# Attention block with SwiGLU: per-group storage of queries and keys, earlier first maxima, a three-tile operation order and a GpSimd split of the maxima

## The chip, the cores and the metric

The kernel runs on one NeuronCore of a Trainium2 chip. The metric is the device time of one execution in microseconds; before the change the median of three runs is 2182.06 us (2181.04 to 2183.07).

The engines named below are TensorE (PE in the profile; its weight loads are PEld), VectorE (DVE), ScalarE (ACT), GpSimd (POOL) and SyncE (SP, which here only issues DMAs).

## The reference

One pre-norm transformer block on 2048 tokens of width 640, with 32 heads of 20 dimensions and a SwiGLU feed-forward of width 1728, all in float32:

```python
h  = x + attention(layernorm(x)) @ wo        # qkv = layernorm(x) @ wqkv; scores * 20 ** -0.5; softmax
h2 = h + (silu(n @ w_gate) * (n @ w_up)) @ w_down      # n = layernorm(h)
```

The softmax subtracts the row maximum. The output is `h2`, 1 x 2048 x 640.

## The kernel before, in words

**Precision.** Most matrix products are made from float32r operands that are split into a high part and a remainder (`split`: ScalarE rounds, VectorE or GpSimd subtracts). A projection is then the sum of three products.

**Projection stage.** Tokens go in four chunks of 512 (`c` = 0 to 3). Each chunk has 18 slots: ten blocks of 128 query or key dimensions (`query_key`, 15 matmuls of 512 columns each) and eight value parts (`value`, 15 matmuls of 320 columns). The last chunk does its five key blocks, then the values, then its five query blocks. `keep` copies a finished block to the tile `e` (two buffers), splits it there on ScalarE and GpSimd, and stores it to DRAM (`qk_d`) from ScalarE's DMA queue, one block behind. The layernorm of the next chunk runs on VectorE between the slots, and `flip` turns it into `z_hi` and `z_lo`.

**Heads and units.** Heads go in eight groups of four. A unit `u` is one group and one chunk of 512 queries, so there are 32. Two heads of a group lie in the lower 64 partitions and two in the upper (`b` = 0, 1), so a score matmul occupies one half of TensorE's rows. Keys and queries of a group are stacked from `qk_d` by `stack`, four DMAs each on SyncE's queue: `load_keys`, `load_queries`, and `load_staged`, which puts a copy into `raw` tiles for early use.

**Row maxima.** Before a unit's scores can be made, the maximum of each query over all 2048 keys is needed. Each maximum is a score matmul followed by a reduction on VectorE. In the projection stage a wide maximum covers both halves at once (`max_pair`: two matmuls into `ps_wide`, one reduction of 128 x 1024). In the attention stage a single maximum covers one half (`max_one`: one matmul into `ps_max`, three banks, one reduction of 128 x 512). `visit(n)` starts up to `n` wide maxima that are ready at the end of a slot; the lists `urgent` and `early` hold them with the slot from which they are allowed. `rest` lists what is left for the attention stage. There are 168 wide maxima and 1712 single ones.

When a unit's maxima are complete, `max_all` reduces them over the key chunks with the sign turned, and `max_finish` transposes them on TensorE, splits the result into two float32r parts on VectorE and writes these by four DMAs into spare rows of the unit's query tile. The score matmul then subtracts the maximum by itself.

**Attention stage.** Each unit walks over 16 key tiles of 128. A tile makes four scores with exponentials (`scores`: one matmul into `ps_one`, four banks, one activation) and weighs the values of the tile two before (`weigh`). The operations of a tile are an order written out by hand: `s` and `S` are scores of the lower and upper half, `m` and `M` single maxima of the lower and upper half, `W` is the weighting. The order alternates between two tiles, and upper and lower case are exchanged in every second pair.

```python
ORDER = ("ssmSWS", "mMsMsWSmMmS")
```

At the end of a unit, the weighted sums are copied, divided by the row sums and stored (`row_sums`, `reciprocals`, `spread`, `store_o`). The output projections of the first chunks run inside the last two units. The feed-forward stage follows.

Of the kernel before, what the change touches and what calls it, by code (L numbers as in the profile page):

```python
# [14 lines left out]
ALU = mybir.AluOpType  # L15
# [21 lines left out]
EPS = 1e-5  # L37

ORDER = ("ssmSWS", "mMsMsWSmMmS")
# [3 lines left out]
def tile_block(ctx: ExitStack, tc: tile.TileContext, x, wqkv, wo, wg, wu, wd, out):  # L43
# [6 lines left out]
    qk_d = dram.tile([2, 2, D, S], F32R, name="qk_d")  # L50
# [59 lines left out]
    def stack(dst, which, g, cs):  # L110

        src = qk_d[which].bitcast(F32).rearrange("i (d h) c -> (i d) h c", h=H)
        for b in range(2):
            heads = src[:, g * G + b : (g + 1) * G : 2, cs]
# [50 lines left out]
    def max_all(u):  # L165
        ends[u] = stk.tile([P, G * TPC], F32, name="neg", tag="neg", bufs=2)
        nc.vector.tensor_reduce(
            ends[u], mxs[u].rearrange("p b h t k -> p (b h t) k"), axis=AX.X, op=ALU.max,
            negate=True,
        )  # L170

    def max_finish(u):

        m = ps_one()[: G * TPC, :P]
        nc.tensor.transpose(m, ends.pop(u), ident)
        m2 = stk.tile([G * TPC, 2, P], F32R, name="m2", tag="m2", bufs=1)
        nc.vector.tensor_copy(m2[:, 0], m)
        nc.vector.tensor_tensor(out=m2[:, 1], in0=m, in1=m2[:, 0].bitcast(F32), op=ALU.subtract)
        for b in range(2):
            for i in range(2):  # L180
                row = b * ROW + NPART + i
                nc.sync.dma_start(
                    queries[u][row : row + 1].bitcast(F32).rearrange(
                        "r j (t p) -> r (j t) p", t=TPC
                    ),
                    m2[b * 2 * TPC : (b + 1) * 2 * TPC, i, :].bitcast(F32),
                )

# [6 lines left out]
        for kc in range(2 if u == 2 else 1 if u % NC < 2 else 0, NC)  # L195
        for t in range(TPC)
        for pair in range(2)
    ]
# [5 lines left out]
    with tc.tile_pool(name="pa", bufs=2) as pa:  # L204
# [31 lines left out]
        def load_staged(i):  # L236
            g, c = sets[i]
            k, q = stage_tile(), stage_tile()
            stack(k, 1, g, slice(0, CH))
            stack(q, 0, g, slice(c * CH, (c + 1) * CH))  # L240
            staged[i] = q, k

        def load_next(i):
            if i < len(sets):
                if slot[0] + 1 >= ready_at(sets[i][1]):
                    load_staged(i)
                else:
                    waiting_load.append(i)

        def first_keys(i, t, pair):  # L250
            if t == 0 and pair == 0:
                load_next(i + 1)
            max_pair(mxs[sets[i][0] * NC + sets[i][1]], *staged[i], pair, t, 0, 0)
# [6 lines left out]
        def in_unit(u, kc, at):  # L260
            return [
                (at, lambda t=t, pair=pair: unit_keys(u, kc, t, pair))
                for t in range(TPC) for pair in range(2)
            ]

        def in_set(i):
            return [
                (ready_at(sets[i][1]), lambda t=t, pair=pair: first_keys(i, t, pair))
                for t in range(TPC) for pair in range(2)
            ]  # L270

        urgent = [a for kc in range(NC) for a in in_unit(0, kc, 18 * kc + (14 if kc == 0 else 8))]
        early = [a for i in range(NG - 1) for a in in_set(i)]
        early += in_unit(1, 0, ready_at(1))
        early += [a for i in range(NG - 1, len(sets)) for a in in_set(i)]
        early += in_unit(2, 0, ready_at(2)) + in_unit(2, 1, ready_at(2))

        def visit(n):
            if waiting_load and slot[0] + 1 >= ready_at(sets[waiting_load[0]][1]):
                load_staged(waiting_load.pop())  # L280
# [8 lines left out]
        def load_w(i):  # L289

            m, n = blocks[i]
# [53 lines left out]
        def store(*last, queue=nc.scalar):  # L345

            if stores:
                queue.dma_start(*stores.pop())
            if last:
                stores.append(last)  # L350

        def query_key(c, *ms):

            z_hi, z_lo = zs[c]
            pss = [ps_one() for _ in ms]
            n = 0
            for a, w in ((z_hi, w_hi), (z_lo, w_hi), (z_hi, w_lo)):
                for ps, m in zip(pss, ms):
                    for k in range(ND):
                        nc.tensor.matmul(  # L360
                            ps, w[:, k, m * P : (m + 1) * P], a[:, k, :],
                            start=(n == 0 and k == 0), stop=(n == 2 and k == ND - 1),
                        )
                n += 1
            for ps, m in zip(pss, ms):
                keep(c, m, ps)

        def keep(c, m, ps):
            e = evp.tile([P, 2, CH], F32R, name="e")
            split_sbuf(ps, e[:, 0], e[:, 1], e[:, 1].bitcast(F32))  # L370
            dst = qk_d[m // ND].bitcast(F32).rearrange("i r c -> r i c")
            store(dst[(m % ND) * P : (m % ND + 1) * P, :, c * CH : (c + 1) * CH], e.bitcast(F32))

        def value(c, t, half):
# [16 lines left out]
            if half == 1:  # L391
                rows = slice((c * TPC + t) * P, (c * TPC + t + 1) * P)
                store(v_d[rows], ev)
            else:
                store()
# [3 lines left out]
        order = [5, 6, 7, 8, 9, 0, 1, 2, 3, 4, 10, 11, 12, 13, 14]  # L399
        blocks = [(5, 2), (7, 2), (9, 1), (0, 2), (2, 2), (4, 1), (10, 2), (12, 2), (14, 1)]  # L400
# [7 lines left out]
        first_raw = raws.pop(order[0]), raws.pop(order[1])  # L408
        for i, raw in enumerate(first_raw):
            cs = slice(order[i] * P, (order[i] + 1) * P)  # L410
            nc.scalar.activation(w_hi[:, :, cs], raw, AF.Copy)
        for t in range(TPC):
            flip_tokens(t)
        for i, raw in enumerate(first_raw):
            cs = slice(order[i] * P, (order[i] + 1) * P)
# [8 lines left out]
        keys_first = [("block", m) for m in order[:ND]]  # L424
        first = [("block", *order[:2]), ("none",), *keys_first[2:]]
        queries_next = [("block", m) for m in order[ND : 2 * ND]]
        flip_at = (12, 11, 11)
        finish_at = 18 * NC
        for c in range(NC):
            lns = []  # L430
            work = (keys_first if c else first) + queries_next + parts
            if c == NC - 1:
                work = keys_first + parts + queries_next
            for j, (kind, *which) in enumerate(work):
                slot[0] = 18 * c + j
                if c == 0 and j < 9:
                    for i in range(split_at[j], split_at[j + 1]):
                        m = order[i + 2]
                        split_w(m)
                        if loaded < len(blocks) and m == sum(blocks[loaded - 4]) - 1:  # L440
                            load_w(loaded)
                            loaded += 1
# [6 lines left out]
                visit(3)  # L449
                if c == 0 and j == 11:  # L450
                    load_staged(0)
# [3 lines left out]
                if j == (7 if c == 0 else 5):  # L455
                    load_keys(0, slice(c * CH, (c + 1) * CH))
                if j == 10 and c < 3:
                    load_queries(c)
# [193 lines left out]
    todo, tail, accs, closing = [], [], {}, []  # L652
# [21 lines left out]
    for u in range(NU):  # L674
# [4 lines left out]
        for kt in range(NT):  # L679
            ready, closing[:] = closing[:], []  # L680
# [262 lines left out]
```

## Time and profile before

| quantity | value |
|---|---|
| median of three runs | 2182.06 us (2181.04 to 2183.07) |
| the profiled execution | 2184.13 us |
| its span, first to last instruction | 2182.3 us |
| projection stage, to the first exponential | 312.4 us |
| attention stage, first to last exponential | 312.4 to 1565.5 us |
| steady attention unit (16 tiles) | 37.54 to 37.67 us |
| units 0, 1, 30 | 39.7, 38.7, 62.7 us |
| granted TensorE clock | 0.998 |

All durations come from one profiled execution. The time of that execution is 1.8 us above its span and 2.1 us above the median. The busy time of an engine counts an instruction from its start to its modelled end; neighbouring instructions overlap, so the mean duration in a row is longer than the distance at which two of them follow each other. Lines such as L161 are line numbers of the kernel before.

### The profile page before, as it was taken

Reading aid. Unit: us, or ns where it says so; the run is one execution under the profiler, and the core shown is the slowest. Engines: PE = TensorE matmul, PEld = TensorE weight load, DVE = VectorE, ACT = ScalarE, POOL = GpSimd, SP = SyncE. Lnnn points to the kernel's source line nnn. Section 1 sums busy time; section 2 is a strip of 40 time slices with the busy share of each in tenths; the row PEclk is TensorE's granted clock in tenths of the full one; section 3 lists DMA queues with packets and bytes.
Section 4 is the critical chain, followed back from the end, with each engine's and each line's share of the span. In section 5 each row is a group of like instructions: output and inputs, shape, how many; then the busy total and the mean of one; then the engine's idle time right before and its main releaser. Section 6 shows DMA issues by size and latency. Waiting matters only on the chain.

```text
span 2182.3 us, 33646 instructions
## 1 busy us (share of the span) xinstructions
PE 2148.1 (98%) x12882; PEld 1250.8 (57%) x12882; DVE 1640.5 (75%) x2835; ACT 1312.8 (60%) x2454; POOL 302.6 (14%) x218
## 2 busy tenths in 40 slices
PE   7999999999999999999999999999999999999999
PEld 5776763333333333333333333345688888888888
DVE  6699879999999999999999999974353343453444
ACT  4322238999999999999999999976622111121110
POOL 5222220000000000000000001011213222122220
PEclk9999999999999999999999999999999999999999
DMA  6555421211102102112111012011221000010102
GB/s 205 193 174 196 162 99 30 58 36 55 47 22 62 43 19 78 27 41 64 34 57 45 24 58 77 19 58 57 73 63 40 25 25 25 19 31 19 31 19 97
DMA packets 120864, 136.60 MB, mean 63 GB/s; under 512 B 37440, under 2 KB 71104, under 8 KB 120704
## 3 DMA queue, kind: packets, MB, share of 16 engines
q1 hardware_dynamic: 107600, 107.71, 17.0%
q10 hardware_dynamic: 13104, 26.75, 3.4%
q8 instruction: 101, 1.65, 0.3%
q14 instruction: 59, 0.48, 0.1%
HBM read 95.62 MB, written 38.01 MB: 61 GB/s over the span
## 4 chain that ended last, share of the span: by engine, by line
PE 88%; DVE 6%; DMA 4%; ACT 1%; issue 0%; SPq 0%; POOL 0%; ACTq 0%; DVEq 0%; POOLq 0%
PE acc L610 22%; PE ps_one L600 18%; PE ps_a L794 17%; PE ps_max L155 11%; PE ps_b L880 9%; PE ps_one L360 4%; DVE mx L161 2%; DVE mx L149 2%; DMA qk_d<-e 2%; PE ps_one L382 2%; PE ps_max L540 2%; PE ps_wide L145 2%; PE ps_b L540 1%; ACT e L217 0%; DMA wo_raw<-in_A_wo 0%
## 5 line engine op out<-in xcount | busy, mean ns | idle before, releaser
L606 ACT ACTIVATE probs<-ps_one 128x512 f32<-128x512 f32 x2048 | 1080.7, 601 | 142.5 <-PE ps_max L155 86.8
L161 DVE TENSOR_REDUCE mx<-ps_max 128x1 f32<-128x512 f32 x1712 | 1067.4, 683 | 64.7 <-PE ps_max L155 58.5
L600 PE MATMUL ps_one<-q_stk,k_stk 62*128 62x512 f32 x2048 | 682.6, 445 | 2.6 <-ACT probs L606 1.0
L155 PE MATMUL ps_max<-k_stk,q_stk 60*128 60x512 f32 x1712 | 609.4, 439 | 4.7 <-DVE mx L161 1.5
L600 PEld LDWEIGHTS ps_one<-q_stk,k_stk 62*128 62x128 f32 x2048 | 338.1, 184 | 413.5 <-ACT probs L606 362.8
L610 PE MATMUL acc<-probs,v_stk 128*32 128x512 f32 x4096 | 547.0, 606 | 0.0
L885 DVE TENSOR_TENSOR h<-ps_b,h 128x320 f32<-128x320 f32 x448 | 194.6, 486 | 311.9 <-PE ps_b L880 311.8
L155 PEld LDWEIGHTS ps_max<-k_stk,q_stk 60*128 60x128 f32 x1712 | 277.8, 185 | 142.2 <-DVE mx L161 119.9
L794 PE MATMUL ps_a<-z,gu_hi 128*128 128x512 f32 x1080 | 276.0, 393 | 0.6 <-ACT z L71 0.6
L794 PEld LDWEIGHTS ps_a<-z,gu_hi 128*128 128x128 f32 x1080 | 200.4, 188 | 42.2 <-ACT z L71 0.8
L149 DVE TENSOR_REDUCE mx<-ps_wide 128x2 f32<-128x1024 f32 x168 | 194.6, 1219 | 33.2 <-PE ps_wide L145 32.8
L71 ACT ACTIVATE y_hi<-s 128x512 fp32r<-128x512 f32 (+1 forms) x56 | 35.4, 631 | 253.9 <-DVE s L807 247.5
L645 POOL TENSOR_TENSOR o<-o,rb 128x512 f32<-128x512 f32 x31 | 39.8, 1284 | 1032.0 <-DMA q_stk<-qk_d 642.7
L610 PEld LDWEIGHTS acc<-probs,v_stk 128*32 128x32 f32 x4096 | 80.7, 108 | 157.7 <-issue 149.5
L802 ACT ACTIVATE s<-ps_a 128x512 f32<-128x512 f32 (+1 forms) x56 | 33.5, 598 | 199.4 <-PE ps_a L794 199.4
L794 PE MATMUL ps_a<-z,gu_lo 128*128 128x512 f32 x540 | 142.2, 393 | 0.0
L880 PE MATMUL ps_b<-d_hi,y_hi 128*128 128x320 f32 x448 | 139.0, 311 | 0.0
L880 PE MATMUL ps_b<-d_lo,y_hi 128*128 128x320 f32 x448 | 138.1, 309 | 0.0
L880 PE MATMUL ps_b<-d_hi,y_lo 128*128 128x320 f32 x416 | 128.3, 308 | 0.0
L217 ACT ACTIVATE e<-ps_one 128x512 f32<-128x512 f32 x55 | 32.9, 598 | 150.4 <-DMA qk_d<-e 74.6
L794 PEld LDWEIGHTS ps_a<-z,gu_lo 128*128 128x128 f32 x540 | 101.4, 188 | 23.1
L72 POOL TENSOR_TENSOR y_lo<-s,y_hi 128x512 fp32r<-128x512 f32 x52 | 67.8, 1303 | 269.6 <-ACT y_hi L71 269.6
(109 smaller groups left out, 1535.4 us busy)
## 6 DMA issues: line engine op xcount, KB each, us to landing
qk_d<-e ACTq DMA_DIRECT2D x39, 512.0 KB
k_stk<-qk_d SPq DMA_DIRECT2D x64, 160.0 KB
q_stk<-qk_d SPq DMA_DIRECT2D x64, 160.0 KB
raw<-qk_d SPq DMA_DIRECT2D x56, 160.0 KB
rb<-r_d SPq DMA_DIRECT2D x32, 256.0 KB
v_d<-ev ACTq DMA_DIRECT2D x16, 384.0 KB
v_stk<-v_d SPq DMA_DIRECT2D x28, 192.0 KB
xt<-in_A_x SPq DMA_DIRECT2D x16, 320.0 KB
```

What stands on the lines that cost most here:

```text
L72: lo_engine.tensor_tensor(out=lo, in0=src, in1=hi.bitcast(F32), op=ALU.subtract)
L149: nc.vector.tensor_reduce(mx[:, :, pair, t, kc], ps, axis=AX.X, op=ALU.max)
L155: nc.tensor.matmul(ps, queries[u][rows, pair, t * P : (t + 1) * P], keys[u // NC][rows, pair, kc * CH : (kc + 1) * CH], start=True, stop=True,
L161: nc.vector.tensor_reduce(mxs[u][:, b, pair, t, kc : kc + 1], ps, axis=AX.X, op=ALU.max)
L360: nc.tensor.matmul(ps, w[:, k, m * P : (m + 1) * P], a[:, k, :], start=(n == 0 and k == 0), stop=(n == 2 and k == ND - 1),)
L540: nc.tensor.matmul(ps[:, :HALF], a[:, k, :], w[:, k, hs], start=(n == 0), stop=(n == 3 * ND - 1),)
L600: nc.tensor.matmul(ps, keys[u // NC][rows, p, kt * P : (kt + 1) * P], queries[u][rows, p, :], start=True, stop=True,)
L606: nc.scalar.activation(probs[p][:, b, :], ps, AF.Exp, scale=scale)
L610: nc.tensor.matmul(acc[32 * j : 32 * j + 32, :], values[u // NC][:, kt, j * VW : j * VW + 32], probs[j // 2][:, j % 2, :], start=(kt == 0) ...
L794: nc.tensor.matmul(ps, a[:, i, k, :], b[:, k, :], start=(n == 0), stop=(n == 3 * ND - 1))
L880: nc.tensor.matmul(ps[:, :HALF], a[:, t * P : (t + 1) * P], b[:, hs], start=(n == 0), stop=(n == len(products) - 1),)
L885: nc.vector.tensor_tensor(out=h, in0=ps[:, :HALF], in1=h, op=ALU.add)
```

## The change

1. `qk_d` is laid out by head group, so that a group's 80 query or key dimensions are contiguous. The columns of `wqkv` are permuted on the host to match, and query and key blocks alternate. A block of 128 dimensions then lies in two or three groups and is stored in two or three pieces.
2. The first wide maxima are allowed from slot 6 instead of 14, per group (`ready_at`). `visit` is called with two in the middle of a block and two after it, instead of three after it; value slots keep three. Unit `c = 1` of each group also does part of its second key chunk early (`in_projections`). Staged sets are 21 instead of 14. In the built program there are 208 wide maxima and 1632 single ones.
3. In chunk 0 every third block uses `third`, a view of the value tile, as an additional `e` buffer.
4. The attention order has three tiles, without the exchange of case; when no maxima are left it is `sSsSW`. Finished maxima are transposed two tiles after they close instead of one.
5. The split of a finished maximum happens before the transpose on GpSimd (`max_all`: a copy and a subtraction of 128 x 16); after the transpose one ScalarE copy takes the place of the two VectorE operations.

```diff
-ORDER = ("ssmSWS", "mMsMsWSmMmS")
+GD = G * DH
+ORDER = ("SmsSMMsWMm", "SsSmWmMs", "SssMWmS")
...
-    qk_d = dram.tile([2, 2, D, S], F32R, name="qk_d")
+    qk_d = dram.tile([2, NG, 2, GD, S], F32R, name="qk_d")
...
     def max_all(u):
-        ends[u] = stk.tile([P, G * TPC], F32, name="neg", tag="neg", bufs=2)
+        neg = stk.tile([P, G * TPC], F32, name="neg", tag="neg", bufs=2)
         nc.vector.tensor_reduce(
...
+        ends[u] = stk.tile([P, 2, G * TPC], F32R, name="both", tag="both", bufs=2)
+        nc.gpsimd.tensor_copy(ends[u][:, 0], neg)
+        nc.gpsimd.tensor_tensor(
+            out=ends[u][:, 1], in0=neg, in1=ends[u][:, 0].bitcast(F32), op=ALU.subtract
+        )
     def max_finish(u):
-        nc.tensor.transpose(m, ends.pop(u), ident)
-        m2 = stk.tile([G * TPC, 2, P], F32R, name="m2", tag="m2", bufs=1)
-        nc.vector.tensor_copy(m2[:, 0], m)
-        nc.vector.tensor_tensor(out=m2[:, 1], in0=m, in1=m2[:, 0].bitcast(F32), op=ALU.subtract)
+        nc.tensor.transpose(m, ends.pop(u).bitcast(F32).rearrange("p i n -> p (i n)"), ident)
+        m2 = stk.tile([2 * G * TPC, P], F32R, name="m2", tag="m2", bufs=1)
+        nc.scalar.activation(m2, m, AF.Copy)
...
+    def in_projections(u, kc, t):
+        g, c = divmod(u, NC)
+        if u == 0 or (u == 2 and kc < 2) or (c < 2 and kc == 0):
+            return True
+        return c == 1 and kc == 1 and t < (2 if g < NG // 2 else 3)
...
-        sets = [(g, c) for c in range(2) for g in range(1, NG)]
-        def ready_at(c):
-            return 18 * c + 14
+        sets = [(g, 0, 0) for g in range(1, NG)]
+        sets += [(g, 1, kc) for g in range(1, NG) for kc in range(2)]
+        def ready_at(g, c):
+            block = ((g + 1) * GD - 1) // P
+            return 2 * block + 6 if c == 0 else 18 * c + 9 + block
...
         def query_key(c, *ms):
...
+                        if n == 1 and k == 3:
+                            visit(2)
...
         def keep(c, m, ps):
-            e = evp.tile([P, 2, CH], F32R, name="e")
+            if c == 0 and m % 3 == 2:
+                e = third.bitcast(F32R)
+            else:
+                e = evp.tile([P, 2, CH], F32R, name="e")
...
-                visit(3)
+                visit(2 if kind == "block" else 3)
...
-                closing.append(a[0])
+                closing[a[0]] = now[0] + 2
...
-            for op in ORDER[kt % 2]:
-                if kt % 4 >= 2 and op != "W":
-                    op = op.swapcase()
+            order = ORDER[now[0] % 3] if singles[0] or singles[1] else "sSsSW"
+            for op in order:
```

More of the change, by code (lines that the diff above doesn't have):

```diff
@@ L194, in tile_block @@
         for u in range(1, NU)
-        for kc in range(2 if u == 2 else 1 if u % NC < 2 else 0, NC)
+        for kc in range(NC)
         for t in range(TPC)
         for pair in range(2)
+        if not in_projections(u, kc, t)
     ]
@@ L244, in load_next, with load_waiting @@
             if i < len(sets):
[L245 to L248, printed above, removed]
+                waiting_load.append(i)
+                load_waiting()
+        def load_waiting():
+            if waiting_load and slot[0] + 1 >= ready_at(*sets[waiting_load[0]][:2]):
+                load_staged(waiting_load.pop())
         def first_keys(i, t, pair):
@@ L252, in first_keys @@
                 load_next(i + 1)
-            max_pair(mxs[sets[i][0] * NC + sets[i][1]], *staged[i], pair, t, 0, 0)
+            g, c, kc = sets[i]
+            max_pair(mxs[g * NC + c], *staged[i], pair, t, kc, 0)
         def unit_keys(u, kc, t, pair):
@@ L345, in store @@
         def store(*last, queue=nc.scalar):
[L347 to L350, printed above, removed]
+            while stores:
+                queue.dma_start(*stores.pop(0))
+            stores.extend(last)
         def query_key(c, *ms):
@@ L392, in value @@
                 rows = slice((c * TPC + t) * P, (c * TPC + t + 1) * P)
-                store(v_d[rows], ev)
+                store((v_d[rows], ev))
             else:
@@ L407, in tile_block @@
             f()
[L408 to L411, printed above, removed]
+        first_raw = raws.pop(0), raws.pop(1)
+        for m, raw in enumerate(first_raw):
+            nc.scalar.activation(w_hi[:, :, m * P : (m + 1) * P], raw, AF.Copy)
         for t in range(TPC):
             flip_tokens(t)
-        for i, raw in enumerate(first_raw):
-            cs = slice(order[i] * P, (order[i] + 1) * P)
+        for m, raw in enumerate(first_raw):
+            cs = slice(m * P, (m + 1) * P)
             nc.vector.tensor_tensor(
@@ L423, in tile_block @@
         parts = [("value", *divmod(i, 2)) for i in range(2 * TPC)]
-        keys_first = [("block", m) for m in order[:ND]]
-        first = [("block", *order[:2]), ("none",), *keys_first[2:]]
-        queries_next = [("block", m) for m in order[ND : 2 * ND]]
+        first = [("block", 0, 1), ("none",)] + [("block", m) for m in range(2, 2 * ND)]
+        some_keys = [("block", 2 * i) for i in range(ND)]
+        some_queries = [("block", 2 * i + 1) for i in range(ND)]
         flip_at = (12, 11, 11)
@@ L437, in tile_block @@
                     for i in range(split_at[j], split_at[j + 1]):
-                        m = order[i + 2]
-                        split_w(m)
-                        if loaded < len(blocks) and m == sum(blocks[loaded - 4]) - 1:
+                        split_w(i + 2)
+                        if i % 2 == 1 and loaded < 8:
                             load_w(loaded)
@@ L650, in store_o @@
             )
-    todo, tail, accs, closing = [], [], {}, []
+    todo, tail, accs, closing, now = [], [], {}, {}, [0]
     singles = [[(*a, b) for a in rest] for b in range(2)]
```

73 lines of the change are left out of this document (44 added, 29 removed).

## The prediction

> **What bounds the kernel now.** I read the totals first, then the busy time stage by stage, then single starts inside the two stages that the diff touches. The feed-forward stage (from 1565.5 us on) keeps its instructions and is taken as unchanged.
>
> ```profile
> span 2182.3 us, 33646 instructions
> ...
> PE 2148.1 (98%) x12882; PEld 1250.8 (57%) x12882; DVE 1640.5 (75%) x2835; ACT 1312.8 (60%) x2454; POOL 302.6 (14%) x218
> ```
>
> Busy time by stretch (columns: span, PE, PEld, DVE, ACT, POOL, clock, DMA share, GB/s): two token chunks of the projections, 30 attention units, units 30 and 31.
>
> ```profile
> 84.50:162.60 78.10, 76.10 (x399) 56.23 (x399) 72.72 (x85) 21.86 (x38) 19.35 (x15) 1.00 0.56 181
> 162.60:239.40 76.80, 75.39 (x400) 55.98 (x399) 72.40 (x85) 21.97 (x38) 19.34 (x15) 1.00 0.56 183
> 312.40:1446.00 1133.60, 1129.47 (x7457) 430.36 (x7453) 1070.15 (x1798) 1030.49 (x1957) 54.79 (x38) 1.00 0.17 47
> 1446.00:1508.70 62.70, 60.02 (x366) 32.88 (x364) 37.22 (x84) 39.05 (x79) 7.60 (x5) 1.00 0.16 50
> 1508.70:1565.50 56.80, 56.70 (x340) 31.13 (x341) 16.93 (x47) 38.66 (x78) 7.58 (x5) 1.00 0.11 32
> ```
>
> In both stages TensorE (PE) and VectorE (DVE) are both nearly full. Moving maxima forward therefore relieves one full stage and loads another. The timeline (start, length, count) within one old two-tile cycle shows what holds attention:
>
> ```profile
> 703.11 1.06 PE L610 MATMUL acc<-probs,v_stk 128*32 128x512 f32 x8
> 704.11 0.49 PE L600 MATMUL ps_one<-q_stk,k_stk 62*128 62x512 f32 x1
> 704.11 1.11 PE L155 MATMUL ps_max<-k_stk,q_stk 60*128 60x512 f32 x3
> 704.72 1.20 PE L600 MATMUL ps_one<-q_stk,k_stk 62*128 62x512 f32 x4
> ```
>
> VectorE beside it:
>
> ```profile
> 702.78 4.38 DVE L161 TENSOR_REDUCE mx<-ps_max 128x1 f32<-128x512 f32 x7
> 707.42 2.58 DVE L161 TENSOR_REDUCE mx<-ps_max 128x1 f32<-128x512 f32 x4 [0.26 <-PE ps_max L155]
> ```
>
> VectorE runs seven reductions back to back, then starves. TensorE waits too: the third maximum behind the weighting at 703.11 starts at 704.72, when the reduction begun at 703.98 gives back one of three `ps_max` banks. Both idle in turn because the old order puts one maximum into one tile and six into the next.
>
> **Attention, steady tiles.** Starts of single rows give the rules. Weighting (W) to the next matmul takes 1.00 us, the first step to the second 0.34, later steps 0.235, the last step to W 0.32. A step holds one matmul on each row half (s, m lower; S, M upper), since neighbours on different halves start together. Reductions follow at 0.60 and begin 0.56 after an interval's first matmul; a bank is free 0.75 after its reduction begins. Exponentials follow at 0.48.
>
> Old order, without waits: three steps (1.00 + 0.34 + 0.235 + 0.32 = 1.90) and five steps (2.37), so 4.27 for two tiles. Measured, W to W, are 1.90 and 2.74 (703.11 to 705.85), sum 4.64: 0.38 is the bank wait with the weight load that it exposes (0.11).
>
> New order, W to W: `m S, S m, s S, M, M s` is five steps, 2.37; `M m, S s, S m` three, 1.90; `m M, s S, s, s M` four, 2.13. Sum 6.40 for three tiles, 2.13 a tile: TensorE's own work per tile is as before. Maxima per interval are 4, 3 and 3 instead of bunched. The fourth in the long interval is the one that waits: the first has its matmul at 1.00, its reduction at 1.56, its bank back at 2.31, where the fourth could start at 2.05. That is 0.26, plus up to 0.11 of exposed weight load. Three in the other intervals find free banks (the third of the last comes at 1.81, its bank 0.3 earlier). VectorE needs 10 x 0.60 = 6.0, ScalarE 12 x 0.48 = 5.8: neither is the bound. I take 6.70, between 6.66 and 6.77.
>
> A unit is 16 tiles: 16/3 x 6.70 = 35.7. Old units take 37.65, which is 8 x 4.64 + 0.52; I keep the 0.52 though two VectorE operations (L177 and L178, 0.28 each) leave it. New unit 36.2, a gain of 1.45 x 30 units = **43 us**. Bounds: no waits at all (34.6) 92 us; old rate kept 2 us.
>
> The ScalarE copy that replaces those operations has no row: 0.20 (the one-column activation L471) to 0.60 (L217), I take 0.3, 9 us over 31 units in a stage where ScalarE idles 103; the exponentials queue behind it and have four banks of cover. The two small GpSimd operations are bounded by nothing and 1.3 us (its 512-column rows): GpSimd is busy 55 of 1134 us, and the transpose now comes two tiles (4.5 us) after the last maximum, so I take zero. If GpSimd were late, the transpose on TensorE and everything behind it would stand. Each unit's rows still arrive in time: unit 1 has 40 single maxima left, closes in tile 11, is transposed in tile 13, needed in tile 16; four DMA issues of 0.65 and a landing fit into that.
>
> **Attention, last two units.** After the maxima end (tile 489, both orders) the new order is `sSsSW`. With an output projection (2.40) a tile takes 1.00 + 2.40 + 0.34 + 0.32 = 4.06; the old pair took 9.06 (W at 1508.92, 1517.98). Eight tiles gain 3.8. Some 14 light tiles go from 2.13 towards the exponentials' 1.92: 2.5. Unit 30's eight projection tiles with maxima go from 5.14 (1456.51 to 1466.78 for two) to about (6.40 + 7.2 + 0.9)/3 = 4.83: 2.4. Together **9 us**, bounds 3 to 13.
>
> **Projections: 40 wide maxima more (168 to 208), 80 single ones fewer.**
>
> ```profile
> L149 DVE TENSOR_REDUCE mx<-ps_wide 128x2 f32<-128x1024 f32 x168 | 194.6, 1219 | 33.2 <-PE ps_wide L145 32.8
> ```
>
> One slot of the timeline (start, length):
>
> ```profile
> 87.51 0.62 PE L360 MATMUL ps_one<-z_hi,w_lo 128*128 128x512 f32 x2
> 88.06 0.96 PE L145 MATMUL ps_wide<-raw 60*128 60x512 f32 x6
> ...
> 92.60 0.97 PE L145 MATMUL ps_wide<-raw 60*128 60x512 f32 x6
> ```
>
> VectorE takes a wide maximum every 1.14. A block slot here (88.06 to 92.60) is 4.55: 15 matmuls at 0.229, three wides at 0.229, and 0.40 for entering and leaving half-array matmuls. Four wides in two visits make 3.44 + 0.92 + 0.80 = 5.16. The built order has 88 such excursions against 56. TensorE's price is 40 x 0.229 + 32 x 0.40 = 22 us.
>
> The Trainium skill ("TensorEngine Tiling (Array Packing)", Key Properties) says that changing the tiling mode drains TensorE, which speaks against splitting the visits. The rows show it cheaper than a full drain: the wide at 88.06 starts before the end of the matmul ahead (87.51 + 0.62 = 88.13). Waiting for both ends would make 0.53 an excursion and 4 us more; no run here shows such a wait, and the sum below uses the rows.
>
> By chunk, wides are 12, 54, 54, 48 before and 40, 60, 64, 44 after. In chunks 1 and 2 VectorE is the fuller engine once wides are added (72.7 + 6.8, 72.4 + 11.4 busy), so these grow by **7 and 11**. Chunk 0 gets 28 more: four block slots at about 5.9 (four wides 4.56, plus weight splits and layernorm steps that took 0.6 to 2.2 each there) and eight value slots at 3.6, less the 4.8 that TensorE waited for stores, which a third `e` buffer ends: end near 91 instead of 84.5, **+6.5**. Chunk 3 has four fewer wides but more excursions, and five final blocks at the pace of their stores:
>
> ```profile
> ACT e L217 <- DMA qk_d<-e: 74.6, 23, 4.7
> ```
>
> (us, times, longest, from 16 to 312 us.) In the chain, the landing of a staged load and of a store:
>
> ```profile
> 147.89 3.13 DMA raw<-qk_d
> ...
> 304.85 2.75 DMA qk_d<-e
> ```
>
> A store becomes two or three pieces, 96 issues against 40, 0.37 each on ScalarE's queue, with the next copy behind them: harmless at a 5.2 slot, up to 0.5 a block in the tail. Chunk 3: **+4.5**.
>
> Staged sets are 21 instead of 14, 56 more issues of 0.34 on SyncE. A set's eight issues and a landing of 3.1 make 5.8. Eight wides last 10 us and hide it; three sets of four wides last 5.2 and miss by 0.6; four sets of six hide it. **+2**; with the longest landing in the chain (6.2) 15 instead. Sum **+31**. Low end 17: TensorE's 22 less 4.8. High end 46.
>
> **Sum.** 31 - 43 - 9 = -21. The profiled execution (2184.1, span 2182.3) would become 2163; it lies 2 above the median of 2182.1, so the median becomes **2161**.
>
> **Rivals.**
> *Bank waits vanish.* For: 4/3/3 spacing, VectorE at 6.0 of 6.4. Against: three banks, four maxima in one interval. 31 - 92 - 9 = -70: 2112. Chance 0.12.
> *Wides cost only TensorE's share* (visits spaced so that VectorE never holds it): 17 - 52 = -35: 2147. Against: VectorE at 94% in chunk 2 already. Chance 0.12.
> *Staged loads late.* DMA already moves 181 GB/s in these chunks and SyncE's queue is in order, so a load that waits for a store holds those behind it. With landings of 6.2: -8; a little more brings it level: 2174 to 2182. Chance 0.12.
> *Slower: scores wait for their banks.* The long interval issues five scores in 1.3 us into four `ps_one` banks; the fourth needs the bank of the last score before W, free at 1.78, where it could start at 1.58. That is hidden behind the maximum's wait only while ScalarE keeps pace. From 0.2 more in each cycle (6.93) attention returns no more than the projections take; at the old rate, 2.32 a tile, it is 31 - 2 - 9 = +20: 2202. For: exponentials run 10 to 15% short of bound, so any copy queued ahead shows. Chance 0.13.
> The counts (208 and 1632) stand in the built order, so a change that does not do what it says is given nothing.
>
> **How the numbers follow.** The forecast case keeps 0.51, itself 2150 to 2175. 0.2% is 4.4 us, about what a measurement of this kernel can tell from no change. Faster by more: the forecast's 0.51, 0.12 + 0.12, and 0.04 of the late loads: 0.79. Same: the other 0.08. Slower: 0.13. The range leaves out part of each outer case: 2122 to 2190.
>
> **What would show it.** Right: attention starts near 343 instead of 312; units of 36.2; W-to-W of about 2.7, 1.9 and 2.1; VectorE above 94% of chunks 1 and 2. Wrong: units above 37.2, with score matmuls waiting for ScalarE; wide maxima waiting for `raw` loads more than 10 us in total; transposes waiting for GpSimd.

## The result: slower by 1.0%, and the profile after

The changed kernel takes 2206.61 us (median of four runs, 2199.24 to 2207.58) against 2182.57 for the kernel before: ratio 1.0102, 95% interval 1.0089 to 1.0114. The forecast, 2161 with a range to 2190, had the wrong sign. The profiled execution is the fastest of the four, 2199.24 us with a span of 2197.5, and so 15 above that of before. The profile can explain these 15; the other 9 between the medians it does not show (the other three executions were granted a mean TensorE clock of 0.987 to 0.989, the profiled one 0.990).

The totals of the changed kernel, then its busy time by stretch (columns as in the prediction): chunks 1 and 2 of the projections, units 0 to 29, units 30 and 31.

```profile
span 2197.5 us, 33889 instructions
...
PE 2140.9 (97%) x12882; PEld 1258.5 (57%) x12882; DVE 1613.8 (73%) x2731; ACT 1278.1 (58%) x2486; POOL 317.0 (14%) x282
```

```profile
94.80:188.40 93.60, 84.58 (x413) 59.34 (x412) 78.05 (x91) 21.85 (x38) 19.87 (x16) 0.95 0.53 161
188.40:285.00 96.60, 87.06 (x421) 59.53 (x420) 83.24 (x94) 21.97 (x38) 19.51 (x15) 0.94 0.55 169
...
366.20:1467.70 1101.50, 1097.41 (x7374) 430.39 (x7372) 1006.97 (x1660) 995.80 (x1985) 66.82 (x98) 0.99 0.17 48
1467.70:1528.00 60.30, 57.82 (x370) 33.33 (x373) 34.62 (x79) 38.61 (x80) 8.52 (x7) 1.00 0.16 47
1528.00:1579.10 51.10, 51.10 (x340) 28.37 (x342) 16.91 (x47) 37.64 (x77) 7.61 (x5) 1.00 0.14 41
```

Read against the rows of before, stage by stage. Units 0 to 29 went from 1133.6 to 1101.5 us (forecast -43, measured -32.1), units 30 and 31 from 119.5 to 111.4 between the ends of their rows, -8.3 by the exponentials (forecast -9). Both chunks of the projections grew, from 78.1 and 76.8 to 93.6 and 96.6, where +7 and +11 were forecast, and neither engine is full there any more: VectorE (third busy column) is at 83% and 86%, where above 94% was a sign of being right, TensorE at 90%, and its mean clock is 0.95 and 0.94 instead of 1.00. The first exponential comes at 366.2 instead of 312.4: +53.8, forecast +31. The feed-forward stage adds 1.6. Together that is the +15.1 between the spans, but for rounding.

| stage, us | forecast | measured |
|---|---|---|
| to the first exponential | +31 | +53.8 |
| units 0 to 29 | -43 | -32.1 |
| units 30 and 31 | -9 | -8.3 |

In the timeline of one new three-tile cycle the weightings show the intervals, and VectorE's row its run of reductions:

```profile
699.83 1.06 PE L646 MATMUL acc<-probs,v_stk 128*32 128x512 f32 x8
...
702.57 1.06 PE L646 MATMUL acc<-probs,v_stk 128*32 128x512 f32 x8
...
704.10 3.19 DVE L162 TENSOR_REDUCE mx<-ps_max 128x1 f32<-128x512 f32 x5 [0.26 <-PE ps_max L156]
...
704.47 1.06 PE L646 MATMUL acc<-probs,v_stk 128*32 128x512 f32 x8
...
706.60 1.06 PE L646 MATMUL acc<-probs,v_stk 128*32 128x512 f32 x8
```

2.74, 1.90 and 2.13 us from weighting to weighting: 6.77, the upper bound of the forecast's 6.66 to 6.77. The wide maxima are there too, as forecast:

```profile
L150 DVE TENSOR_REDUCE mx<-ps_wide 128x2 f32<-128x1024 f32 x208 | 240.4, 1217 | 34.8 <-PE ps_wide L146 34.3
```

What the forecast did not expect is who waits. In the list of waits from 16 to 366 us (us, times, longest), wide maxima wait for staged loads for 12.9 us; more than 10 was one of the prediction's signs of being wrong. The third line is that of the kernel before, from 16 to 312 us:

```profile
ACT e L232 <- DMA qk_d<-e: 75.3, 17, 5.7
...
PE ps_wide L146 <- DMA raw<-qk_d: 12.9, 10, 4.6
```

```profile
PE ps_wide L145 <- DMA raw<-qk_d: 0.3, 1, 0.3
```

The length of a slot is read from the end of the last matmul of the slot before to the end of its own last matmul. Two slots are the longest of all in the changed kernel, the last of chunk 1 with 11.30 us (3.29 before) and the third of chunk 2 with 11.42 (4.55 before); they are "the two late slots" below. In the chain of the same stretch, the last of six issues of staged loads in a row and the landing behind it at the end of chunk 1, and the landing of a store ahead of the first exponential:

```profile
178.62 0.74 SPq L118
179.40 3.88 DMA raw<-qk_d
...
360.60 3.46 DMA qk_d<-e
```

And each issue of a staged load takes SyncE twice as long as before, the loads of 160 KB and of 80 KB alike. The instructions that touch `raw`, of the kernel before, of the changed kernel and of experiment e1 (duration in ns: least, median, longest):

```profile
L117 SPq DMA_DIRECT2D raw<-qk_d x112: 273/335/1814, 68.5 to 257.7; - x112
```

```profile
L118 SPq DMA_DIRECT2D raw<-qk_d x168: 738/742/1523, 40.1 to 301.9; - x168
```

```profile
L118 SPq DMA_DIRECT2D raw<-qk_d x168: 273/336/2099, 39.3 to 294.6; - x168
```

### The profile page after: what moved, and what is told of

It is laid out like the page before. It is cut to its first block, busy times and chain, and to the rows that moved or that the text cites. A ratio compares the mean times of both kernels' runs of the same rounds, so it can differ in the third digit from the quotient of the medians.

```text
span 2197.5 us, 33889 instructions
## 1 busy us (share of the span) xinstructions
PE 2140.9 (97%) x12882; PEld 1258.5 (57%) x12882; DVE 1613.8 (73%) x2731; ACT 1278.1 (58%) x2486; POOL 317.0 (14%) x282
## 4 chain that ended last, share of the span: by engine, by line
PE 88%; DMA 4%; DVE 4%; SPq 1%; ACT 1%; issue 1%; POOL 0%; ACTq 0%; POOLq 0%; DVEq 0%
PE acc L646 23%; PE ps_a L830 17%; PE ps_max L156 15%; PE ps_one L636 13%; PE ps_b L916 9%; PE ps_one L381 3%; PE ps_one L422 2%; DVE mx L150 2%; PE ps_wide L146 2%; DMA raw<-qk_d 2%; PE ps_max L576 2%; PE ps_b L576 1%; SPq L118 1%; DMA qk_d<-e 1%; DVE mx L162 0%
## 5 line engine op out<-in xcount | busy, mean ns | idle before, releaser
L642 ACT ACTIVATE probs<-ps_one 128x512 f32<-128x512 f32 x2048 | 1044.7, 621 | 136.2 <-PE ps_one L636 135.4
L162 DVE TENSOR_REDUCE mx<-ps_max 128x1 f32<-128x512 f32 x1632 | 1020.4, 682 | 113.2 <-PE ps_max L156 77.9
L636 PE MATMUL ps_one<-q_stk,k_stk 62*128 62x512 f32 x2048 | 552.5, 423 | 6.6 <-ACT e L232 5.6
L156 PE MATMUL ps_max<-k_stk,q_stk 60*128 60x512 f32 x1632 | 543.4, 462 | 1.9 <-DVE mx L162 1.3
L156 PEld LDWEIGHTS ps_max<-k_stk,q_stk 60*128 60x128 f32 x1632 | 231.7, 185 | 431.7 <-DVE mx L162 412.6
L636 PEld LDWEIGHTS ps_one<-q_stk,k_stk 62*128 62x128 f32 x2048 | 301.3, 186 | 85.0 <-ACT probs L642 51.9
L150 DVE TENSOR_REDUCE mx<-ps_wide 128x2 f32<-128x1024 f32 x208 | 240.4, 1217 | 34.8 <-PE ps_wide L146 34.3
L173 POOL CAST both<-neg 128x16 fp32r<-128x16 f32 x32 | 6.6, 207 | 834.5 <-DVE neg L169 393.4
```

What stands on the lines that cost most here:

```text
L150: nc.vector.tensor_reduce(mx[:, :, pair, t, kc], ps, axis=AX.X, op=ALU.max)
L156: nc.tensor.matmul(ps, queries[u][rows, pair, t * P : (t + 1) * P], keys[u // NC][rows, pair, kc * CH : (kc + 1) * CH], start=True, stop=True,
L162: nc.vector.tensor_reduce(mxs[u][:, b, pair, t, kc : kc + 1], ps, axis=AX.X, op=ALU.max)
L636: nc.tensor.matmul(ps, keys[u // NC][rows, p, kt * P : (kt + 1) * P], queries[u][rows, p, :], start=True, stop=True,)
L642: nc.scalar.activation(probs[p][:, b, :], ps, AF.Exp, scale=scale)
```

## Experiments

Below, "start" is the time of the first exponential in the profile, which ends the projections; it is read beside the time of the whole, since a second edit may act in attention. A start comes from one execution: e13 and e16, which run the same program up to the last chunk, end chunk 2 at 269.2 and 274.7 us, so a start alone is good to some 5 us. Ratios are to the kernel before, measured again with each group of runs; its medians there are 2182.5 to 2184.8.

### The slow issues, and the order of the tiles

A stack's load names 40 rows of two heads. With heads d-major inside a group and `b::2` taken, 40 x 2 equidistant rows look in DRAM like one dimension of 80, while the target keeps 40 x 2: source and target no longer have the same shape. This follows from the strides in the kernel; the profile lists the shape of the target alone. e1 puts the heads 0, 2, 1, 3 in DRAM, so that the pair lies side by side and both sides read 40 x 2 x 512 again:

```
-            heads = src[:, b::2, cs]
+            heads = src[:, 2 * b : 2 * b + 2, cs]
-  reshape(D, 2, NG, G, DH).transpose(0, 1, 2, 4, 3)
+  reshape(D, 2, NG, 2, 2, DH).transpose(0, 1, 2, 5, 4, 3)
```

> The changed kernel, with the four heads of a group stored in another order (0, 2, 1, 3), so that the two heads a stacking DMA takes lie next to each other and its source keeps the same 40 x 2 x 512 shape as its target. Theory A (the stacking DMAs cost SyncE 0.74 us each instead of 0.34 because source and target differ in shape, 80 x 512 against 40 x 2 x 512, and staged loads come late): issue back to 0.34 us, first exponential near 343 us instead of 366, the unit that loads wo (43.7 us) near 38.5, span 2197.5 - 23 - 5 = about 2170. Theory B (VectorE and the extra half-array excursions make the projections long, the loads only wait beside them): issue may fall, but the first exponential stays beyond 357 us and the span above 2188.

Measured: 2192.48, ratio 1.0041 (1.0027 to 1.0054). The issue is back at 0.336, start 358.3. So the slow issues cost 8 us of the start and about 14 of the median; they are not the whole. Unit 27, which was expected near 38.5, stays at 43.61.

e2 is e1 with the old two-tile order, thinned to the same 20 maxima in six tiles.

> As e1_heads, with the two-tile attention order of the kernel before, from which one maximum is dropped in every third pair of tiles so that it too takes 20 maxima in 6 tiles. Same counts, other spacing. If the spacing of the maxima is what shortened the units (37.65 to 36.43 us): units of 37.1 to 37.5 and a time 20 to 32 us above e1_heads. If the smaller number of maxima per tile (3.33 against 3.5) did it: units of 36.3 to 36.6 and within 6 us of e1_heads.

Measured: 2229.81, ratio 1.0214; steady units of 37.50 (37.63 before, 36.43 in the changed kernel), unit 30 64.44. With as few maxima and the old bunching a unit is as long as before: what shortens it is the spacing, as the prediction had it. The order is worth 37 us against e1 by the medians; between the two profiles units 0 to 29 differ by 29 us and the last two units, which lose `sSsSW` with it, by 10.

### What the pieces cost, on the kernel before

e3 is the kernel before with the new layout of `qk_d` alone: grouped rows, stores in pieces, slow issues. e4 is e3 with the head order of e1. e6 leaves layout and loads as they were and only cuts the stores:

```
 cuts = sorted({r0, r0 + P, *(r for r in range(0, D, G * DH) if r0 < r < r0 + P)})
 store(*((dst[a:b, :, ...], e[a - r0 : b - r0]) for a, b in zip(cuts, cuts[1:])))
```

> The kernel before, with the per-group layout of qk_d alone (columns permuted on the host, blocks stored in two or three pieces; block order, visits, attention order as before). Theory A: each stacking DMA costs SyncE 0.74 us; the sets of eight wide maxima last 10 to 12 us and nearly cover 8 x 0.74 + 4, so the projections grow by 2 to 10 us and the unit that loads wo by 3 to 5: 2186 to 2197 in all. Theory B: no slower than 2186.

> As e3_layout_only with the heads of a group stored as 0, 2, 1, 3. Theory A: issue 0.34 us and the time within 3 us of the kernel before, what is left being the store pieces on ScalarE's queue in the tail (up to 2 us). Theory B: the same time as e3_layout_only.

> The kernel before, in its old layout and order, with each block's store cut at the same rows as in the changed kernel (two or three DMAs instead of one, 96 instead of 40 in all). Theory S1 (the number of pieces alone costs the time: their issues and landings lengthen the turn of the two e buffers past a block slot): first exponential 333 to 337, 2202 to 2208, as e3. Rival S2 (it is where the pieces are written, or the loads that wait for them): as the kernel before, 2182 to 2186, first exponential 312 to 316.

Measured: e3 2205.76 (1.0106), start 336.0; e4 2208.62 (1.0119), start 336.9 with issues of 0.335; e6 2201.52 (1.0076, 1.0058 to 1.0094), start 333.2. The attention stage did not change in any of them. So in the old loop the number of pieces alone puts off the start by 21 of the 24 us, wherever they are written (by the medians, each against its own kernel before, 17 of 23), and the slow issues cost nothing. Theory A missed in both e3 and e4: e3 is beyond its 2197, and e4 with fast issues did not come back. The waits of e6 (74.6 us before):

```profile
ACT e L217 <- DMA qk_d<-e: 102.6, 26, 5.8
```

A store is issued behind the next block's copy and its buffer comes back after the landing; with two buffers this turn outgrows the old slot of 4.55 us. That reading rests on these waits; a third buffer in the old loop was not run.

### The same question in the changed kernel

e7 gives e1 the third `e` buffer in the first three chunks (`if c < 3 and m % 3 == 2`). e5 stores every block whole again, into grouped rows without a group dimension; a half stack then needs three loads instead of two, 252 issues instead of 168.

> e1 with the third e buffer used in the first three chunks instead of the first alone; stores in pieces. If a block's copy waits because its e buffer is not yet stored (S1), chunks 1 and 2 shorten by most of the waits e <- DMA: 8 to 15 us off e1, 2178 to 2184, first exponential 343 to 350. If the pieces cost by holding ScalarE's queue, or if the staged loads hold these chunks, nothing changes: 2190 to 2195, first exponential 356 to 360.

> The changed kernel with the head order of e1, but queries and keys kept in the old rows of DRAM (grouped rows, no group dimension): each block is stored by one DMA again, and each half of a stack is loaded by three DMAs instead of two. Theory S (the store pieces cost 24 us, as e3 and e4 show on the kernel before): the 24 come back, first exponential near 335, about 2169. Rival L (in the changed kernel the late staged loads hold the same slots that the stores hold, and each stack now has six issues of 0.34 instead of four): at most 8 come back, first exponential above 350, 2184 or more.

Measured: e7 2196.34 (1.0058, 1.0038 to 1.0077), start 364.8. The waits that it was to remove are removed (70.1 us in e1), and nothing is gained:

```profile
ACT e L232 <- DMA qk_d<-e: 25.9, 6, 5.8
```

e5: 2205.71 (1.0101), start 379.0, slower than e1 although its stores are whole; its `e` waits are down to 21.1. Both say that in the changed kernel, whose slots are 5.2 us, the stores are not what decides; e5 also points to what does, since its other edit is more loads.

e8 is e5 with one visit of four wide maxima behind each block instead of two visits of two.

> e5 with the wide maxima of a block slot in one visit of four behind the block, instead of two of two. If TensorE's price of entering and leaving (0.40 an excursion) decides, 33 fewer excursions give 10 to 13 us: about 2157, first exponential near 323. Rival: three wide banks and a reduction of 1.14 hold the fourth wide maximum of a visit by about 1 us, a block slot grows by more than the 0.40 it saves: 10 to 25 us slower than e5, 2180 to 2195.

Measured: 2234.04 (1.0226), start 406.4, 28 us slower than e5. The split visits pay: without them a plain block slot grows from 5.2 to 5.9.

### Why the staged loads are late

The trace gives each DMA's completion semaphore: the DMAs of SyncE and ScalarE share eight of them in turn, and an issue waits until the DMA that had its semaphore before has landed. In e1 loads stand 54 us on SyncE for a store's semaphore, for instance at 179.2 us for a store of values issued at 173.7. e9 moves each slot's stores behind its visits in the program; e12 lets GpSimd issue them, whose DMAs take other semaphores (`queue=nc.gpsimd`).

> e1 with each slot's stores issued after the slot's visits instead of before them: ScalarE's own order is the same (a visit has none of its work), but a visit's staged loads now come ahead of that slot's stores in the program. Theory Q (each DMA takes one of eight completion semaphores in turn, whichever queue issues it, so a load on SyncE that comes behind a store stands until that store has landed; in e1 such waits are 54 us on SyncE): they drop below 25 us, the staged loads' late slots (21 us in e1) to under 10, first exponential 343 to 350, 2178 to 2185. Rival D (the loads are late because eight issues and a landing do not fit into a set of four): first exponential 355 to 360, 2189 to 2195.

> e1 with all stores of the projections issued by GpSimd instead of ScalarE. In e1 and e9 a load on SyncE waits for the landing of the store that used its completion semaphore before (54 us in all); GpSimd's DMAs take their semaphores from another set. Theory Q (these waits make the staged loads late): the late slots around the chunk ends (9.7 and 12.6 us) fall to 4 to 6, first exponential 340 to 350, 2174 to 2184. Rival D (too much is loaded for a set of four, whoever waits): those slots stay at 9 or more, first exponential 355 or more, 2189 or more. Rival G (issuing costs GpSimd more than it costs ScalarE, and GpSimd's subtractions are in the store's turn): slots grow evenly above 5.2, first exponential above 362.

Measured: e9 2190.34 (1.0037), start 359.5, the waits for stores' semaphores still 54 us: that reordering did nothing, and tells nothing. e12: 2226.26 (1.0198), start 393.8. There these waits are gone, and the two late slots are still 8.75 and 8.87 us (9.65 and 12.63 in e1): shorter, but late. The time is lost elsewhere, in the turn of the stores through GpSimd:

```profile
ACT e L232 <- DMA qk_d<-e: 163.8, 27, 9.2
```

e13 takes e1 and loads less: a set of the second key chunk has the queries of the set before it, so it keeps them. The same kernel splits the output weights one tile later (below).

```
+            if kc:
+                staged[i] = staged[i - 1][0], k
+                return
             q = stage_tile()
```

> e1 in which a set of the second key chunk takes the queries that the set before it has loaded (the same ones) instead of loading them again: seven sets have four loads (480 KB) instead of eight (960 KB or less). And the output weights' splits come one tile later, as in e10 (5 us, read in that unit). Theory D (eight issues and a landing do not fit into a set of four): the late slots at the chunk ends fall to 4 to 7, first exponential 342 to 350, 2172 to 2180. Theory Q: four loads still meet a store's semaphore half of the time: first exponential 350 to 357, 2180 to 2187.

> e13 with the stores of e12. If the two causes are separate their gains add: first exponential 330 to 340, 2162 to 2172, below the kernel before. If they are one wait seen from two sides, it is as the better of the two.

> The changed kernel itself with one edit: the sets of the second key chunk keep the queries of the set before them, as in e13. Head order and so the issues of 0.74 stay. If the volume of the staged loads is the larger part of what the projections took beyond the forecast, first exponential falls from 366 to 350 to 357 and the time to 2185 to 2195. If the slow issues hold the loads whatever their number, first exponential stays above 361 and the time above 2199.

Measured: e13 2174.26, ratio 0.9959 (0.9947 to 0.9972): faster than the kernel before. Start 348.9, the two late slots 4.71 and 6.12. Chunks 1 and 2 and the wait for staged loads:

```profile
94.40:181.40 87.00, 82.83 (x412) 58.00 (x412) 78.29 (x91) 21.95 (x38) 19.80 (x16) 0.96 0.54 166
181.40:269.20 87.80, 83.71 (x420) 57.52 (x420) 83.73 (x94) 21.96 (x38) 19.27 (x15) 0.98 0.58 174
```

```profile
PE ps_wide L146 <- DMA raw<-qk_d: 1.4, 2, 1.0
```

The chunks are at +8.9 and +11.0 over before, where +7 and +11 were forecast. e14, both edits: 2218.51 (1.016); its two slots are 4.59 and 5.20, but GpSimd's stores cost it the rest. e15, the changed kernel with this one edit and the slow issues kept: 2184.27, ratio 1.0005 (0.9995 to 1.0015), start 357.5. Its rows for chunks 1 and 2:

```profile
94.40:183.80 89.40, 83.92 (x413) 58.43 (x412) 77.64 (x91) 21.95 (x38) 19.90 (x16) 0.96 0.52 162
183.80:276.10 92.30, 85.73 (x420) 58.98 (x420) 83.53 (x94) 21.96 (x38) 19.34 (x15) 0.94 0.54 166
```

Twenty-eight loads left out bring the changed kernel level with the one before: 9 us of the start and 22 of the median, against 8 and 14 for the slow issues. What was loaded for the sets of four to six maxima was the larger cause. Whether it acts by its bytes, by its 28 issues (0.74 each in the changed kernel, 0.34 in e1) through the fewer `raw` tiles that it needs or through the shared semaphores is not separated: e12 brought a cost of its own, and the waits for stores' semaphores do not follow the start (25 us in the kernel before, 28 in the changed one, 42 in e13, 24 in e15).

### Unit 27, the tail and the first maxima

Unit 27, which loads the output weights, takes 43.70 us against 39.22 before. The timeline of ScalarE, then of TensorE, in the changed kernel:

```profile
1374.80 0.74 ACT L72 ACTIVATE wo_hi<-wo_raw 128x640 fp32r<-128x640 f32 x1 [3.48 <-DMA wo_raw<-in_A_wo]
```

```profile
1376.17 0.27 PE L181 MATMUL ps_one<-ident,both 128*32 128x128 f32 x1 [3.27 <-ACT probs L642]
```

The split is queued ahead of the exponentials two tiles after its load in the program; the load is not there, ScalarE stands 3.48 us, and TensorE behind it 3.27. In the kernel before this split waited 1.15. Counted from the start of the unit, ScalarE now reaches it at 20.7 us instead of 21.3, since tiles are shorter, and SyncE issues the load at 18.5 instead of 15.9: in the chain it stands behind the stacking loads with their issues of 0.74. With fast issues (e1) it comes at 17.0, lands later, and ScalarE still stands 3.84. e10 splits one tile later, and gives the last five blocks raw tiles as `e` buffers, on e9. e11 adds a later start of the first group's maxima (slot 8 instead of 6). e16 is e13 with the last blocks but one stored right behind their own copies; e17 adds the later start to it.

> e9 and two small edits that are read in stages of their own. The last five blocks put their results into free raw tiles instead of the two e buffers: if the copies wait there for stores, the 7.0 us from the last projection matmul to the first exponential become 1.5 to 3; else they stay. In the unit that loads the output weights each split comes one tile later than now: if ScalarE, whose queue is in order, waited there for the load, the unit takes 37 to 39 us instead of 43.6; if the unit is long for other work, it stays above 42. Together 8 to 11 us off e9.

> e10 with the first group's first wide maxima from slot 8 of chunk 0 instead of slot 6. In e1 slots 6 and 7 take 17.8 us instead of 10.4, waiting for the first loads of queries and keys. If this wait is simply taken out, chunk 0 ends 4 to 7 us earlier and so does all that follows. Rival: the eight wide maxima that leave these slots come back where VectorE is full (chunks 1 and 2), and first exponential moves by less than 2.

> e13 with the stores of the last blocks but one issued right behind their own copies, not behind the next block's. If the wait of 5.4 us ahead of the first score is the turn of the two e buffers (copy, next copy, issues, landing), it falls to 1 to 3 and the time to 2170 to 2172. If the landings themselves are longer than two slots of 3.43, it stays: 2173 to 2176.

> e16 with the first group's maxima from slot 8, as in e11. There chunk 0 gained 4 us that the staged loads took back in chunks 1 and 2. If the loads were the reason, the 4 us now stay: 2166 to 2169. If it is VectorE, which has the same wide maxima to do later, nothing is gained over e16.

Measured: e10 2184.31 (1.0012), unit 27 38.39: that half is settled. Its other half failed: the time from the last projection matmul to the first exponential stays (7.5 against 7.0); TensorE waits only 0.7 for the copies there, but the first exponential stands 6.2 on ScalarE. e11 2188.94 (1.0024), start 358.6: chunk 0 ends 4.2 us earlier than in e10 and the start is where it was. e16 2175.43 (0.9963), start 352.7: no gain, TensorE still stands 4.5 us there. Its chain shows what took the place of the turn of the buffers. The issues now stand right behind their own block on ScalarE, so two copies start 4.09 us apart (347.15 and 351.24), with the rounding (0.64), GpSimd's subtraction (1.27) and three issues (0.31 to 0.46) between them, while a block of TensorE's there lasts 3.43. e17 2168.92, ratio 0.9941 (0.9929 to 0.9953), start 346.5: the fastest of all, 14 us below the kernel before. The later start pays once the loads are fewer, as expected; of the tail 4.4 us remain (1.5 before), with the same chain as in e16. No run takes it apart.

## Why the prediction was wrong, step by step

**Projections, "+2" for the staged loads.** This is the step that failed. It had "56 more issues of 0.34 on SyncE" and let sets of four miss by 0.6 us. The issues became 0.74 with the new places of the heads in DRAM: 8 us of the start (e1; e15 against e13 shows 8.6). And the sets of four to six were late by far more than 0.6: 9 us of the start for queries loaded a second time (366.2 to 357.5, e15). By the medians the two are worth 14 and 22. An estimate from the rows gives the size: eight issues of 0.74 and the landing of 3.88 make 9.8, against the 5.2 that a set of four lasts, so 4.6 short, which is also the longest wait of a wide maximum for a staged load. The rival "staged loads late" named the mechanism and priced it at 15 us with landings of 6.2; that 6.2 was the landing of a store at 25 us, while the staged load in the chain landed in 3.13 before and 3.88 after. The landings hardly grew; the issues ahead of them did. The rival stopped at level, because it did not add the slow issues or the tail.

**Chunk 0, "+6.5".** Too small: it ends at 94.8 instead of 84.5, +10.3, and in e13 too at 94.4. Slots 6 and 7, the first with wide maxima, take 17.0 us together; in the chain a store's landing of 5.60 (from 39.32 us) and the first loads behind it stand there. With the first maxima from slot 8 chunk 0 is some 4 us shorter (e11 against e10; 92.6 in e17).

**The stores, "harmless at a 5.2 slot, up to 0.5 a block in the tail".** The first half holds for the changed kernel (e7), and its slots are longer: at the old 4.55 the same pieces put off the start by 21 to 24 us (e3, e4, e6). The second half was too small: last projection matmul to first exponential went from 1.5 to 6.9 us, +5.4, where the forecast had some 2.5 for five blocks. The pieces alone bring 2.9 of this in the old loop (4.4 in e6); the rest is not taken apart.

**TensorE's and VectorE's price of the wide maxima, 22 of the 31.** Right. A plain block slot is 5.20, forecast 5.16, and with the loads mended (e13) chunks 1 and 2 are at +8.9 and +11.0, forecast +7 and +11. Of the 36.5 us by which the start of e13 is later than before, the other 16.6 are chunk 0 (+9.9) and chunk 3 with the tail (+6.7). The Trainium skill ("TensorEngine Tiling (Array Packing)", Key Properties) has a change of tiling mode drain TensorE. With a full wait, which the prediction priced at 0.53 for each of two visits, a slot would last 5.42; the trace does not bear that out.

**Half clock, not in the forecast.** The trace of the clock has stretches at half speed: 12.8 us in the kernel before, 44.4 in the changed one, 29.5 in e13. In the changed kernel, behind the start, TensorE has seven gaps of 2.0 to 5.6 us, and each has such a stretch beginning 3.2 to 4.4 us after the gap began. Length alone does not decide: in e1 two gaps of 2.14 and 2.26 have none, and in the kernel before 6.8 us at half clock follow where no gap is above 0.98. At half clock projection matmuls start every 0.427 instead of 0.229, so 31.6 us more of it cost up to 31.6 x (1 - 0.229/0.427) = 15 where nothing else is the bound. A late load can so be paid a second time; this lies inside the other terms of this list, not beside them, and no run separates it. The Trainium skill ("TensorE: Matmul & The Clock Gate", Part 1) names an idle window of about 3.4 us for the drop; here a gap of 2.39 us at 45.8 us is followed by 3.4 us at half clock.

**Attention, "-43".** The mechanism was right and the size off. The cycle is 6.77 instead of 6.70 and a steady unit 36.43 instead of 36.2: 0.23 x 28 = 6.4 us. Unit 27 stands 7.3 above its neighbours instead of 1.6: 5.7 us, a wait of 3.3 on TensorE with 6.8 us at half clock behind it (from 1376.9), which the forecast did not look for. Units 0 and 1 together gave 1.1 more than the forecast's 1.45 each, which leaves the 11 that are missing. **Units 30 and 31, "-9"**: 2.5 and 5.8, right. **GpSimd and the ScalarE copy**: 0.20 and 0.22 us for the two GpSimd instructions, 0.27 for the copy (0.3 forecast); hidden as forecast, as far as the units of 36.43 show. **Slower, by scores that wait for banks**: did not happen, the attention stage gained; the slower result came from the projections.

## What to carry to other kernels

Count a prefetch by its slowest consumer: sets that shrink from eight maxima to four halve the time that hides a load, while the load shrank only from 960 to 720 KB here, so first ask what two neighbouring sets could share. When a layout changes, write out the dimensions of both sides of each DMA as they are issued; issue time (0.34 or 0.74 us here) and the number of pieces changed with them, and both acted outside the stage that was looked at. A load two tiles ahead of its use in the program is only as early as its queue lets it be: in unit 27 its issue came 2.6 us later and its use 0.6 earlier.

## What the runs showed of the hardware

An issue of the same 160 KB load took a median of 0.33 us on SyncE where, by the strides, source and target are 40 x 2 x 512 (e1, e4) and 0.742 us with a source of 80 x 512 against that target (the changed kernel, e3); only the places of the heads in DRAM differ between e3 and e4, and between the changed kernel and e1. In the old loop this was hidden entirely (e3 and e4 have the same start), in the new one it cost 8 us of the start. SyncE and ScalarE took turns with eight completion semaphores, and in e1 SyncE stood 54 us until stores of ScalarE's queue had landed. A store moved from ScalarE's queue to GpSimd's more than doubled the waits for its buffer, from 70.1 us to 163.8 (e12).
